# Rounding a kernel's weights two pieces at a time, turning one batch's exponentials through memory, and a new order of clamps and exponentials

## Chip, cores and metric

The kernel runs on one core of one Trainium2 chip. The metric is device microseconds of that core for one execution, the median of several runs. The engines are named PE (TensorE), DVE (VectorE), ACT (ScalarE), POOL (GpSimd) and SP (SyncE, here the queue that issues the DMAs). Each engine works through its own instructions in the order in which they are written, and waits only for data and buffers.

## What is computed

An attention block between 512 tokens and 32 state rows (8 batches, 8 heads of 64), and then a feed-forward block with a gelu over all 8 x 544 rows:

```python
scores = scale * x @ state^T;   a = softmax(scores);    xread = a @ state
scores2 = scale * state @ x^T;  a2 = softmax(scores2);  sread = a2 @ x
rows = concat([xread, sread])            # 4352 rows of 512
h = rows @ w_in                          # 512 -> 2048
g = h * (1 / (1 + exp(-1.702 * h)))
out = g @ w_out                          # 2048 -> 512
```

The arrays w_in and w_out come as 64-bit numbers (the random float32 values divided by a float64 scalar), and the kernel rounds them to float32 itself.

## The kernel before, in words

**Weights.** Both matrices are read as pairs of 32-bit words. They are cut into 32 pieces of 128 x 512 numbers (PIECES, line 180): 16 of w_in, four for each of the four 512-wide blocks w_in[0] to w_in[3], then 16 of w_out, whose pieces come as (row block f, row block f + 8) for f = 4, 5, 6, 7, 0, 1, 2, 3. A piece's raw words (512 KB) land in free rows of w_out itself (pieces 0 to 7 and 12 to 15) or in `later` (all others, room for four), by `load_weight` (184) on the SP queue. A piece is rounded by five DVE instructions of 512 elements and two of ACT: `mask` (216, L221) takes the exponent bits; `round_a` (223, L232 and L233) turns them into a power of two with two Relu on ACT, called the clamp here; `sign` (242, L245) adds the sign; `fraction` (235, L239) takes the high fraction bits; `round_b` (247, L258 and L264) adds the low word and multiplies by the power. `power` rooms are four of the six rows of `low`. Piece 18 alone has its clamp on DVE (L229, L230). `round_to` and `powers_to` say how many pieces are rounded or clamped by a place in the code; `refill` issues the next loads once the raw words in their room have been used.

**Attention.** Batches 0 and 1 are worked together at the start. `att_M(b, c)` (575) multiplies the state with w_in[c], eight PE products of 64 rows x 512 into two PSUM banks, and copies both to SBUF on ACT. `up_x(b, f)` (671, through `up`, 653) makes one 128 x 512 block of h, four PE instructions, and a gelu on ACT (L651) empties its bank; with wait=True the gelu is put on a list that `gelus(n)` (648) issues later. Softmax over the tokens: `two_s_max` (457, DVE), `two_s_exp` (467, four Exp with sums per batch, ACT, written to `room`), `two_s_norm` (485, DVE). For `att_sread` (618, 64 small PE products per batch, L629, scaled on ACT at L635) these exponentials have to be transposed. Batch 0 does it on the PE: `att_eT` (607), eight 128 x 128 transposes (L615) and two ACT copies (L616). Batch 1, and all later batches, go through memory: `eT_out` (592) writes four times 128 KB to a DRAM tile, `eT_in` (597) reads 512 KB back, and `eT_turn` (603, L605) turns 32 x 32 blocks on DVE, twice per batch.

**Banks.** PSUM has four fixed banks, bank_o[0] to bank_o[3], and two rings of two: psA (`att_ps`, tag "att") and psH (tag "h"). A tile of a ring takes a bank over from the tile two allocations before it, once all that read that one are done.

**Down product.** The loop `for i in range(HF)` at the end of the part around the change does eight steps. In step i the two pieces of rows f and f + 8 are needed (`pair_sums`, DVE sums of weights and of gelu outputs, L1479), and seven products P1 to P7 are added up in seven banks (`pair`, L1548, four PE instructions each). In step 0 stand, in this order: P1, sread of batch 0, M(1,2), three left sums, the turns of batch 1, M(1,3), rounding up to piece 19, sread of batch 1, `pair_sums`, P2, one up-product of batch 1 whose gelu is issued at once (`early`, psH), `att_srT` of both batches (a PE transpose and an ACT copy, L640 and L641), clamps up to piece 21, P6. Then P7 and P3 get their banks from psH, P4 and the later up-products from psA, and P5, P7, P3, P4 follow.

The order within each engine is that of the code; nothing else plans it.

Of the kernel before, what the change touches and what calls it, by code (L numbers as in the profile page):

```python
# [10 lines left out]
FP32 = mybir.dt.float32  # L11
# [9 lines left out]
def kernel(  # L21
# [159 lines left out]
    raw, power, begun, signed = {}, {}, {}, {}  # L181
    AHEAD = 3

    def load_weight(i):

        key = PIECES[i]
        nin, room = NFC * NPR, NF // 2
        if i < room or nin - NPR <= i < nin:
            o = 2 * (i % room if i < room else i - (nin - NPR))
            raw[i] = w_out[:, o : o + 2].rearrange("p f n -> p (f n)").bitcast(I32)  # L190
        else:
            o = 2 * (i % 4)
            raw[i] = later[:, o : o + 2].rearrange("p f n -> p (f n)").bitcast(I32)
        if key[0] == "i":
            _, c, k = key
            src = w_in_words[P * k : P * (k + 1), 2 * FC * c : 2 * FC * (c + 1)]
        else:
            src = w_out_words[P * key[1] : P * (key[1] + 1)]
        nc.sync.dma_start(raw[i], src)
# [16 lines left out]
    def mask(i):  # L216

        _, hi = words(i)
        sc = low[:, 2 + i % (AHEAD + 1)].bitcast(I32)
        power[i] = sc  # L220
        nc.vector.tensor_scalar(sc, hi, 0x7FF00000, None, ALU.bitwise_and)  # L221

    def round_a(i):

        if i not in power:
            mask(i)
        sc = power[i]
        if i == NFC * NPR + 2:
            nc.vector.tensor_scalar(sc, sc, most, least, ALU.min, ALU.max)  # L229
            nc.vector.tensor_scalar(sc, sc, -least, 8.0, ALU.add, ALU.mult)  # L230
            return
        nc.scalar.activation(out=sc.bitcast(FP32), in_=sc, func=AF.Relu, bias=edge[0], scale=-8.0)  # L232
        nc.scalar.activation(out=sc, in_=sc.bitcast(FP32), func=AF.Relu, bias=edge[1], scale=-1.0)  # L233

# [52 lines left out]

    def round_to(n, ahead=AHEAD):

        nin = NFC * NPR  # L290
        while done["b"] < min(n, len(PIECES)):
            i = done["b"]
            powers_to(i + 1)
            round_b(i, min(i + 1 + ahead, i + 3 if i > nin + 3 else i + 2 if i >= nin else nin), i >= nin or i + 1 < nin and (i + 1 < n or i >= NPR))
            done["b"] += 1
            refill()

    def piece(fill):
# [5 lines left out]
        refill()  # L304

    def pace(pieces):

        done["credit"] += pieces
        n = int(done["credit"])
        done["credit"] -= n  # L310
        round_to(done["b"] + n)


# [153 lines left out]
    def two_s_exp(b, room):  # L467
        a = A[b]
        sm = a["sm2"] = apool.tile([P, NG, 2], FP32, tag="sm4", name=f"sm4_{b}", bufs=2)
        a["e2"] = [(room[:, g], sm[:, g, :1]) for g in range(NG)]  # L470
        for g in range(NG):
            if b:

                dst = room[:, g].rearrange("p (v k i a) -> p i k v a", v=SCH, k=2, i=2)
                view = lambda t: t.rearrange("p (k v a) -> p k v a", k=2, v=SCH)
            else:
                dst = room[:, g].rearrange("p (k i q) -> p i k q", k=2, i=2)
                view = lambda t: t.rearrange("p (k q) -> p k q", k=2)
            for i in range(2):
                nc.scalar.activation(  # L480
                    out=dst[:, i], in_=view(a["s"][i][:, 2 * P * g : 2 * P * (g + 1)]), func=AF.Exp,
                    bias=a["mx2"][:, 0, g : g + 1], scale=scale, accum_out=sm[:, g, i : i + 1],
                )
# [105 lines left out]

    squares = dram.tile([SCH, Ns, NG, NPR, P], FP32, name="squares")  # L590

    def eT_out(b):
        for j in range(NPR):
            src = e2_room[b][Ns * j : Ns * (j + 1)].rearrange("n g (i q) -> n g i q", i=SCH)
            nc.sync.dma_start(squares[:, :, :, j].rearrange("i n g q -> n g i q"), src)

    def eT_in(b):

        a = A[b]
        a["eT"] = apool.tile([P, NG, SCH, P], FP32, tag="e1" if b == 1 else "eT", name=f"eT_{b}")  # L600
        nc.sync.dma_start(a["eT"].rearrange("p g j q -> p (g j q)"), squares.rearrange("i n g j q -> (i n) (g j q)"))

    def eT_turn(b, g):
        t = A[b]["eT"][:, g].rearrange("p c q -> p (c q)")
        nc.vector.transpose(t, t)  # L605

    def att_eT(b, g, spare=False):

        a = A[b]
        if g == 0:  # L610
            a["eT"] = apool.tile([P, NG, SCH, P], FP32, tag="eT", name=f"eT_{b}")
        name = f"eT_{b}_{g}"
        ps = psH.tile([P, SCH, P], FP32, tag="h", name=name) if spare else att_ps([P, SCH, P], name)
        for c in range(SCH):
            nc.tensor.transpose(ps[:, c], a["e2"][g][0][:, P * c : P * (c + 1)], ident)  # L615
        nc.scalar.copy(a["eT"][:, g], ps)  # L616

    def att_sread(b):
# [3 lines left out]
        for g in range(NG):  # L622
            for c in range(SCH):
                for j in range(NPR):
                    st = slice(Ns * j, Ns * (j + 1))
                    e, v = a["eT"][:, g, c, st], xn[b][:, NG * j + g, c]
                    if b:
                        e = a["eT"][:, g, j, Ns * c : Ns * (c + 1)]
                    nc.tensor.matmul(  # L629
# [667 lines left out]

    def rounds(n, *ahead):
        round_to(done["b"] + n, *ahead)


    load_two_states()
# [57 lines left out]
    head_exp(1)  # L1360
    fraction(NPR)
    powers_to(NPR + 2)
    up_x(0, 0, True, wait=True)
# [4 lines left out]
    for g in range(NG):  # L1368
        head_back(1, g, held[g])
    powers_to(NPR + 3)  # L1370
    piece(lambda: fraction(NPR + 1))
    up_x(0, 3, wait=True)
    gelus(2)
    powers_to(2 * NPR)
    piece(lambda: fraction(NPR + 2))
    gelus(2)

    def turn(b, c, then, n=()):

        for i in range(nper):  # L1380
            if i == nper - 1 and then:
                att_M(*then)
            up_x(b, nper * c + i)
            if i < len(n):
                rounds(n[i])

    for i in range(nper):
        up_x(1, i, i > 1, bank_o[i] if i < 2 else None)
        if 0 < i < nper - 1:
            rounds(1, 2 - i)  # L1390
            powers_to(2 * NPR + 1)
    nin = NFC * NPR
    att_M(0, 1, True)
    att_M(1, 1, banks=bank_o[:NG], copied=False)
    powers_to(2 * NPR + 2)
    def up_four(b, f):
        up_x(b, f, bank=bank_o[2 + f % 4 // 2] if f % 2 else None)

    for i in range(nper):
        up_four(0, nper + i)  # L1400
        rounds(1, 0)
        if i == 1:
            M_copies(1, 1)
        powers_to(2 * NPR + 3 + i)
    for i in range(nper):
        up_four(1, nper + i)
        if i == 1:
            att_M(0, 2)
        if i < nper - 1:
            rounds(1, 0)  # L1410
            powers_to(min(3 * NPR + 3 + i, nin))
    powers_to(nin + 1)
    up_four(0, 2 * nper)
    powers_to(nin + 2)
    room = apool.tile([P, NPR, S], FP32, tag="xT", name="e2_01")
    rounds(1, 0)
    two_s_max(1)
    late_banks = [bank_o[2], None, bank_o[3], None, bank_o[0], bank_o[1], bank_o[2]]

    def up_late(f, wait=True):  # L1420
        up_x(0, f, bank=late_banks[f - 2 * nper - 1], wait=wait)

    up_late(2 * nper + 1)
    att_M(0, 3)
    e2_room[1] = room[:, NG:]
    two_s_exp(1, e2_room[1])
    eT_out(1)
    eT_in(1)
    two_s_max(0)
    up_late(2 * nper + 2)  # L1430
    two_s_exp(0, room[:, :NG])
    up_late(2 * nper + 3)
    up_late(3 * nper)
    rounds(2, 1)
    rounds(1, 0)
    for b in (1, 0):
        two_s_norm(b)
    mask(nin + 3)
    up_late(3 * nper + 1)
    gelus(5)  # L1440
    up_late(3 * nper + 2, False)
    up_late(3 * nper + 3, False)
    for g in range(NG):
        att_eT(0, g, True)
    powers_to(nin + 4)

# [115 lines left out]
    for i in range(HF):  # L1562
        round_to(nin + 2 * i + 2)
        gelus(len(waiting))
        if i == 3:
            nc.scalar.copy(G[1, f_early // 2][:, f_early % 2], early)
        if i == 0:
            pair(i, "P1")
            att_sread(0)
            att_M(1, 2, banks=bank_o[1::2])  # L1570
            turns_of(left_sums(0))
            for g in range(NG):
                eT_turn(1, g)
            att_M(1, 3, True)
            round_to(nin + 4, 1)
            att_sread(1)
            t_room.append(pieces(apool.tile([P, NG, SCH * P], FP32, tag="eT", name="t_room_1"), 2, 2))
            s_rooms.append(four(apool.tile([P, NG, NB * Ns], FP32, tag="e1", name="s4_room")))
            pair_sums(i, left_sums(0)[3:])
            pair(i, "P2")  # L1580
            f_early = rest.pop(0)
# [3 lines left out]
            att_srT(1)  # L1585
            powers_to(nin + 6)
            pair(i, "P6")
# [158 lines left out]
```

## Time and profile before

| | us |
|---|---|
| runs | 688.04 median (687.69 to 688.35, 3 runs) |
| the profiled execution | 687.92 |
| its span, first to last instruction | 686.1 |
| PE busy | 676.9 (99%) |
| DVE busy | 558.4 (81%) |
| ACT busy | 328.0 (48%) |
| first step of the down product, P1(0), starts | 72.64 |
| second step, P1(1), starts | 85.23 |

The profile is of one execution. "Busy" is the time in which an engine worked on an instruction. A group line names the source line, the engine, the operation, output and inputs, and a time. In a timeline the first number is the start in us after the span's start, the second how long; "x4" merges that many in a row. A chain of waits goes back from the last instruction to what released each. Times of PE are overlapped by some 0.16 us from one instruction group to the next, so starts are compared and not ends.

### The profile page before, as it was taken

How to read it: one execution, taken by the hardware profiler on the slowest of the kernel's cores; microseconds unless marked ns; L12 is line 12 of the kernel's file. 1: busy time of each engine (PE TensorE's matmuls, PEld its weight loads, DVE VectorE, ACT ScalarE, POOL GpSimd, SP SyncE). 2: the span in 40 equal slices, each digit the busy share in tenths (PEclk: the TensorE clock that was granted, in tenths of full speed). 3: DMA queues.
4: the chain of work that ended last, by engine and by line, in shares of the span. 5: the costliest groups of instructions: out<-in, count | busy, mean ns of one | idle time of the engine just before them, and what ended most of it. 6: DMA issues, size and time to landing. Idle time of an engine off the chain costs nothing.

```text
span 686.1 us, 13606 instructions
## 1 busy us (share of the span) xinstructions
PE 676.9 (99%) x5347; PEld 578.0 (84%) x5347; DVE 558.4 (81%) x1066; ACT 328.0 (48%) x725; POOL 1.5 (0%) x10
## 2 busy tenths in 40 slices
PE   8999999999999999999999999999999999999996
PEld 4443687779988999889988998899988998999995
DVE  6999899999999886988878796888698885986540
ACT  7799844134355443752375335544375237421410
POOL 0000000000000000000000000000000000000000
PEclk9999999999999999999999999999999999999999
DMA  9730545338261754156443645175415640251000
GB/s 320 301 112 25 173 142 144 118 130 267 82 166 69 207 195 115 28 170 190 149 67 117 205 141 112 32 205 196 115 27 170 188 153 1 77 167 49 2 2 30
DMA packets 101391, 88.44 MB, mean 129 GB/s; under 512 B 56656, under 2 KB 80720, under 8 KB 101328
## 3 DMA queue, kind: packets, MB, share of 16 engines
q1 hardware_dynamic: 100784, 87.45, 42.6%
q8 instruction: 42, 0.69, 0.4%
q14 instruction: 21, 0.17, 0.1%
q10 hardware_dynamic: 544, 0.13, 0.1%
HBM read 69.47 MB, written 18.09 MB: 128 GB/s over the span
## 4 chain that ended last, share of the span: by engine, by line
PE 89%; DMA 4%; ACT 3%; DVE 3%; SPq 0%; issue 0%; DVEq 0%; ACTq 0%
PE low L809 28%; PE o L1219 15%; PE o L809 15%; PE upx L1219 6%; PE o L1548 4%; PE M L430 3%; PE down L1548 3%; PE o L708 3%; PE upw L1219 2%; PE o L858 2%; PE down_up L662 2%; PE h L662 1%; PE sr L629 1%; PE o L430 1%; PE upx_sr L1219 1%; ACT low L233 1%
## 5 line engine op out<-in xcount | busy, mean ns | idle before, releaser
L809 PE MATMUL low<-w_out,g_room 128*128 128x128 f32 x416 | 54.3, 276 | 0.0
L809 PEld LDWEIGHTS low<-w_out,g_room 128*128 128x128 f32 x416 | 50.5, 192 | 4.5 <-issue 4.2
L1219 PE MATMUL o<-ta,M 128*128 128x256 f32 x192 | 49.9, 382 | 0.0
L1219 PE MATMUL upx<-aT,M 128*128 128x256 f32 x192 | 49.3, 379 | 0.0
L809 PE MATMUL low<-low,g_room 128*128 128x128 f32 x336 | 43.3, 275 | 0.0
L1219 PEld LDWEIGHTS o<-ta,M 128*128 128x128 f32 x192 | 35.5, 190 | 5.9 <-ACT g_room L1265 1.6
L809 PEld LDWEIGHTS low<-low,g_room 128*128 128x128 f32 x336 | 40.3, 192 | 0.0
L1219 PEld LDWEIGHTS upx<-aT,M 128*128 128x128 f32 x192 | 36.0, 190 | 4.7
L1225 ACT ACTIVATE g_room<-o 128x512 f32<-128x512 f32 (+1 forms) x56 | 31.4, 560 | 10.4 <-PE o L1219 10.4
L809 PE MATMUL low<-sums,later 128*128 128x128 f32 x272 | 34.9, 275 | 0.0
L573 ACT COPY M<-M 128x512 f32<-128x512 f32 x53 | 27.5, 596 | 14.2 <-PE M L430 14.2
L809 PEld LDWEIGHTS low<-sums,later 128*128 128x128 f32 x272 | 32.7, 192 | 0.1
L232 ACT ACTIVATE low<-low,edge 128x512 f32<-128x512 int32 x31 | 22.5, 727 | 20.7 <-DVE low L221 20.7
L865 DVE TENSOR_TENSOR g_room<-g_room 128x512 f32<-128x512 f32 x48 | 31.7, 685 | 0.2
L1219 PE MATMUL o<-ta,ms 128*128 128x256 f32 x120 | 30.8, 379 | 0.0
L1265 ACT COPY g_room<-o 128x512 f32<-128x512 f32 (+1 forms) x28 | 15.6, 556 | 25.3 <-PE o L1219 25.3
L1225 ACT ACTIVATE g_room<-g_room 128x512 f32<-128x512 f32 (+1 forms) x28 | 16.8, 600 | 20.8 <-DVE g_room L1228 20.8
L1219 PEld LDWEIGHTS o<-ta,ms 128*128 128x128 f32 x120 | 22.8, 190 | 3.1
L1219 PE MATMUL o<-aT,m 128*128 128x256 f32 x96 | 24.6, 379 | 0.0
L809 PEld LDWEIGHTS o<-w_out,g_room 128*128 128x128 f32 x160 | 19.4, 192 | 5.0 <-issue 5.0
L430 PE MATMUL M<-w_in,stT 64*32 64x512 f32 x344 | 23.2, 592 | 0.0
L233 ACT ACTIVATE low<-low,edge 128x512 int32<-128x512 f32 x31 | 22.4, 723 | 1.1
(321 smaller groups left out, 1637.6 us busy)
## 6 DMA issues: line engine op xcount, KB each, us to landing
low<-low SPq DMA_DIRECT2D x108, 256.0 KB, 2.5
low<-low SPq DMA_DIRECT2D x11, 768.0 KB, 5.6
later<-in_moe_w_out_dram SPq DMA_DIRECT2D x16, 512.0 KB, 3.5
w_out<-in_moe_w_in_dram SPq DMA_DIRECT2D x12, 512.0 KB, 4.2
xsq<-in_x_dram SPq DMA_DIRECT2D x96, 64.0 KB, 2.2
xn<-in_x_dram SPq DMA_DIRECT2D x12, 512.0 KB, 4.2
out_dram<-osb SPq DMA_DIRECT2D x15, 256.0 KB, 2.2
squares<-e SPq DMA_DIRECT2D x28, 128.0 KB, 2.5
```

Of the source, the lines that this page charges most:

```text
L232: nc.scalar.activation(out=sc.bitcast(FP32), in_=sc, func=AF.Relu, bias=edge[0], scale=-8.0)
L233: nc.scalar.activation(out=sc, in_=sc.bitcast(FP32), func=AF.Relu, bias=edge[1], scale=-1.0)
L430: nc.tensor.matmul(ps[g][st], state_of(b, NG * j + g, g), rhs(rows, j), start=True, stop=True)
L573: nc.scalar.copy(A[b]["M", c][:, g], ps)
L662: nc.tensor.matmul(hps, lhs[i], rhs[i], start=(i == 0), stop=(i == n - 1))
L708: nc.tensor.matmul(ps[:, r], lhs[f][:, P * r : P * (r + 1)], rhs[:, f], start=(first and r == 0 and f == 0), stop=(f == HF - 1), skip_grou ...
L809: nc.tensor.matmul(ps, lhs[f], rhs[:, f], start=(first and f == 0), stop=(f == QF - 1), skip_group_check=True)
L865: nc.vector.tensor_tensor(out=out, in0=x0, in1=x1, op=op)
L1219: nc.tensor.matmul(ps[:, k], lhs[i][:, o : o + P], rhs[i], start=(first and k == 0 and i == 0), stop=(i == n - 1), skip_group_check=True,)
L1225: nc.scalar.activation(out=dst, in_=src, func=AF.Gelu_apprx_sigmoid)
L1265: nc.scalar.copy(c12, Y(u))
L1548: nc.tensor.matmul(ps7[name][:, HN * r : HN * (r + 1)], lhs[:, P * r : P * (r + 1)], rhs, start=(i == 0 and r == 0), stop=(i == HF - 1), s ...
```

## The change

- From piece 4 on, two neighbouring pieces are rounded together: each of the five DVE and two ACT instructions works on 1024 elements. The first four pieces stay single. The clamp of piece 18 on DVE is gone; all are on ACT.
- Batch 0's state exponentials go through memory like batch 1's, into a DRAM tile of their own; the PE transposes and ACT copies are gone. Both batches' maxima, exponentials, writes and reads follow one another, before M(0,3).
- The places of the rounding, of clamps, gelus and bank choices between batch 1's head and the end of the down product's first step are written anew. In step 0 the four turns now stand before the left sums, and the rounding of pair 9 after `pair_sums`, with mask and clamp of pair 10 inside and behind it.

```diff
+    def landing(i):
+        nin, room = NFC * NPR, NF // 2
         if i < room or nin - NPR <= i < nin:
+            return w_out, 2 * (i if i < room else i - (nin - NPR))
+        return later, 2 * (i % 4)
...
+    def pair_room(j):
+        return low[:, 2 + 2 * j % 4 : 4 + 2 * j % 4].bitcast(I32)
...
+    def pair_mask(j):
+        load_weights(2 * j + 2)
+        nc.vector.tensor_scalar(pair_room(j), pair_hi_lo(j)[0], 0x7FF00000, None, ALU.bitwise_and)
+
+    def pair_clamp(j):
+        clamp(pair_room(j))
+        done["a"] = 2 * j + 2
...
+    def round_pair(j, *fills):
+        hi, lo = pair_hi_lo(j)
+        dst, sc = pair_dst(j), pair_room(j)
+        nc.vector.scalar_tensor_tensor(sc, hi, -0x80000000, sc, ALU.bitwise_and, ALU.bitwise_or)
+        nc.vector.scalar_tensor_tensor(dst, lo, 2.0**-32, dst.bitcast(I32), ALU.mult, ALU.add)
+        for fn in fills:
+            fn()
+        nc.vector.scalar_tensor_tensor(dst, dst, 2.0**-20, sc.bitcast(FP32), ALU.mult, ALU.mult)
+        done["b"] = 2 * j + 2
+        raw.clear()
+        refill()
+
+    def round_next(j):
+        round_pair(j, *((lambda: pair_mask(j + 1), lambda: pair_fraction(j + 1)) if 2 * j + 2 < len(PIECES) else ()))
+        if 2 * j + 2 < len(PIECES):
+            pair_clamp(j + 1)
...
-    squares = dram.tile([SCH, Ns, NG, NPR, P], FP32, name="squares")
+    squares = [dram.tile([SCH, Ns, NG, NPR, P], FP32, name=f"squares_{i}") for i in range(2)]
...
+    pair_mask(PAIR + 1)
+    pair_clamp(PAIR + 1)
+    round_pair(PAIR, lambda: pair_fraction(PAIR + 1))
     up_x(0, 3, wait=True)
+    gelus(4)
+    pair_mask(PAIR + 2)
+    round_pair(PAIR + 1, lambda: pair_fraction(PAIR + 2))
+    up_x(1, 0, bank=bank_o[0])
+    up_x(1, 1, bank=bank_o[1])
+    pair_clamp(PAIR + 2)
+    up_x(1, 2, True, wait=True)
+    up_x(1, 3, True, wait=True)
...
     att_M(0, 1, True)
     att_M(1, 1, banks=bank_o[:NG], copied=False)
+    gelus(2)
+    pair_mask(5)
+    round_pair(4, lambda: pair_fraction(5))
+    pair_clamp(5)
+    up_four(0, nper)
+    up_four(0, nper + 1)
+    M_copies(1, 1)
+    pair_mask(6)
+    round_pair(5, lambda: pair_fraction(6))
+    pair_clamp(6)
+    up_four(0, nper + 2)
+    up_four(0, nper + 3)
+    pair_mask(7)
+    round_pair(6, lambda: pair_fraction(7))
+    pair_clamp(7)
+    up_four(1, nper)
+    up_four(1, nper + 1)
+    att_M(0, 2)
+    pair_mask(8)
+    for b in (1, 0):
+        two_s_max(b)
+    up_four(1, nper + 2)
+    pair_clamp(8)
+    up_four(1, nper + 3)
     room = apool.tile([P, NPR, S], FP32, tag="xT", name="e2_01")
+    for i, b in enumerate((1, 0)):
+        e2_room[b] = room[:, NG * i : NG * (i + 1)]
+        two_s_exp(b, e2_room[b])
+        eT_out(b)
+    for b in (1, 0):
+        eT_in(b)
+    round_pair(7, lambda: pair_fraction(8))
+    late_banks = [None, bank_o[2], None, bank_o[3], bank_o[0], bank_o[1], None, None]
...
+    for i in range(3):
+        up_late(2 * nper + i)
     att_M(0, 3)
     up_late(2 * nper + 3)
     up_late(3 * nper)
+    pair_mask(9)
+    round_pair(8, lambda: pair_fraction(9))
     for b in (1, 0):
         two_s_norm(b)
     gelus(5)
+    for i in range(1, nper):
+        up_late(3 * nper + i, False)
+    pair_clamp(9)
...
     for i in range(HF):
-        round_to(nin + 2 * i + 2)
+        if i > 1:
+            round_next(nin // 2 + i)
         gelus(len(waiting))
...
         if i == 0:
             pair(i, "P1")
-            att_sread(0)
             att_M(1, 2, banks=bank_o[1::2])
+            att_M(1, 3, True)
+            for b in (1, 0):
+                for g in range(NG):
+                    eT_turn(b, g)
             turns_of(left_sums(0))
-            for g in range(NG):
-                eT_turn(1, g)
-            att_M(1, 3, True)
-            round_to(nin + 4, 1)
-            att_sread(1)
+            for b in (1, 0):
+                att_sread(b)
...
             pair_sums(i, left_sums(0)[3:])
+            round_next(nin // 2 + 1)
             pair(i, "P2")
             f_early = rest.pop(0)
             early = xn[0].rearrange("p h c d -> p (h c d)")[:, :S]
             up_x(1, f_early, dst=early)
             att_srT(0)
             att_srT(1)
-            powers_to(nin + 6)
             pair(i, "P6")
             ps7["P7"], ps7["P3"] = (psH.tile([P, FC], FP32, tag="h", name=f"down_{k}") for k in (7, 3))
             ps7["P4"], up_bank = (att_ps([P, FC], f"down_{k}") for k in (4, "up"))
```

Pair j holds pieces 2j and 2j + 1: pairs 2 and 3 are w_in[1], 4 and 5 w_in[2], 6 and 7 w_in[3], 8 to 15 those of w_out, one for each step of the down product.

## Prediction

> **What bounds the kernel now.** I read the page's busy slices first, then the waits between 28 and 140 us (the stretch that the change touches), then the chain of waits there, then the instructions in order of time.
>
> ```profile
> PE   8999999999999999999999999999999999999996
> ...
> DVE  6999899999999886988878796888698885986540
> ```
>
> ```profile
> PEld h L662 <- ACT g_room L651: 1.6, 4, 0.8
> DVE eT L605 <- DMA eT<-squares: 1.5, 1, 1.5
> ...
> PEld sr L629 <- DVE eT L605: 1.0, 1, 1.0
> ```
>
> TensorE (PE) is the bound: from 30 us on it is busy in every slice. VectorE (DVE) is full to about 145 us too, but the PE waits for it almost nowhere. So a shorter DVE or ScalarE (ACT) instruction gives nothing by itself; only PE work or PE waits count. The place with the thinnest cover is where state exponentials come back from memory:
>
> ```profile
> 66.01 0.72 SPq L595
> ...
> 68.07 2.59 DMA squares<-e
> ...
> 70.74 5.11 DMA eT<-squares
> 75.85 0.02 issue
> 75.87 0.72 DVE eT L605
> 76.59 0.04 issue
> 76.64 1.25 PE sr L629 x64
> ```
>
> From the last exponential (66.0) to the landing of eT (75.85) are 9.85 us: write and issues 4.7, read 5.1. Next come, on ACT and on PE:
>
> ```profile
> 78.45 0.72 ACT L232 ACTIVATE low<-low,edge 128x512 f32<-128x512 int32 x1 [0.58 <-DVE low L221]
> 79.20 0.72 ACT L233 ACTIVATE low<-low,edge 128x512 int32<-128x512 f32 x1
> ...
> 80.70 0.60 ACT L651 ACTIVATE xn<-h 128x512 f32<-128x512 f32 x1 [0.37 <-PE h L662]
> 81.19 0.43 ACT L641 COPY srT<-srT 128x128 f32<-128x128 f32 x2
> 82.40 0.72 ACT L232 ACTIVATE low<-low,edge 128x512 f32<-128x512 int32 x1 [0.78 <-DVE low L221]
> ```
>
> ```profile
> 78.78 1.88 PE L662 MATMUL h<-low,M 128*128 128x512 f32 x4
> ...
> 82.64 1.03 PE L1548 MATMUL down<-w_out,g_room 128*128 128x256 f32 x4
> 83.51 1.03 PE L1548 MATMUL down<-w_out,s_room 128*128 128x256 f32 x4
> 84.37 1.03 PE L1548 MATMUL down<-t_room,sums 128*128 128x256 f32 x4
> 85.23 1.03 PE L1548 MATMUL o<-w_out,g_room 128*128 128x256 f32 x4
> ```
>
> The reader is to see: the early up-product (h at 78.78) is emptied by the gelu at 80.70, and the two products P7 and P3 (82.64, 83.51) take banks of the same two-bank ring. P3's is the third allocation after the two of M(1,3), so it is the early product's own bank. Here the gelu ends 2.2 us before P3; the clamp of 82.40 is queued behind it. P1 of the second step starts at 85.23, and from there the PE has no wait. That 85.23 is my mark.
>
> [...] one starts 0.60 after the other for L245, L258 and L264, 0.34 for L221 and L239. [...] Trace: the exponential of 1024 took 1.063. [...] Here the read of eT took 5.1 us with three loads behind it, and the first of those (71.18) landed at about 78.0: 6.8.
>
> **The change part by part.**
>
> *Pairs.* Per pair five DVE instructions go: 2 x (3 x 0.60 + 2 x 0.34) = 4.96 becomes 3 x 1.13 + 2 x 0.60 = 4.6; 14 pairs save some 5 us of DVE. A clamp (two Relu) took 1.39 from start to next on ACT; of a pair it takes 1.39 + 0.86 = 2.25 instead of 2.78. All this lies beside the PE: nothing directly. The last pair of each w_in block is ready, added up from 29.67 where head_scale ends, at 38.95 (PE needs it from 39.4), 48.5 (51.4) and 60.95 (61.2 to 61.6). So no wait takes its place.
>
> *Transposes and their copies removed.* Eight PE transposes, 71.77 to 72.64: 0.87 off the path. Two ACT copies (L616) beside the PE.
>
> *PE waits that go.* M(0,3) took 1.56 from start to next instead of 1.01, since w_in was late (0.55); the copies of M(0,1) come sooner because gelus no longer stand before them (about 0.25). So the PE reaches P1(0) at about 71.0 instead of 72.64: 1.65 earlier. The price is paid after that.
>
> *Exponentials earlier.* ACT, added up with the durations above from 30.98: clamp of pair 3, table load and four gelus end at 36.56; clamps 4 to 7 with gelus and copies between them end at 51.7; gelus and copies to 54.6; clamp 8 to 56.9; gelu 57.35; table load 1.28; four exponentials of 2.08 for batch 1 end at 60.75, those of batch 0 at 62.7. Copies of M(0,3) follow to 63.7, just in time for the up-product that needs them (63.8).
>
> *The second turn through memory.* The SP queue holds, in order: 4 writes of batch 1, 4 of batch 0, read 1, read 0, then two weight loads. Writes of batch 1 are issued 60.75 to 63.45; those of batch 0 then, landing 63.45 + 4.7 = 68.15; read 0 is issued there. Alone it would take 5.1 as in the trace. But read 1 went out 2 us before and shares the engines with the last of batch 0's writes (these ran at a DMA share of 0.99 and 194 GB/s in the trace). Bounds: 3.5 (the page's median for a 512 KB load) and 6.8 (the load that had one read in front). I take 5.6: it lands at 73.75. Four DVE turns follow (those of batch 1 done by then), 1.25 for the last two: T = 75.0. DVE had nothing from about 66 to the first landing, since its sums now stand behind the turns.
>
> *The new order after the turns.* This is where the gain is given back. DVE from T: three left sums 2.0 and the pair sums 2.08 (79.87 to 81.95 in the trace), sign 1.13, low word 1.13, mask of pair 10, 0.7: T + 7.04. Only then can ACT clamp pair 10, for 2.25, and this clamp is now queued **ahead** of the early gelu and the srT copies. Gelu ends T + 9.95, P3 starts T + 10.0. The PE itself would be there at T + 6.8 (sread 1.1, P2 0.96, up 1.72, srT 0.31, P6 0.97, P5 and P7 1.73): a wait of 3.2 that the kernel before doesn't have. P3 and P4 take 1.73: P1(1) at T + 11.7 = 86.7, against 85.23. Sum: **+1.5 us**.
>
> *After that.* DVE has the next weights at T + 8.75, T + 14.95 and T + 23.3; the PE wants them at T + 11.7, T + 17.8 and T + 25.5. So no more waits, and what is lost at 85 us is lost at the end, as the PE is full to the end. The profiled execution took 687.92 (span 686.1 and 1.8 around it): 689.4. It stands 0.12 under the median 688.04, so I forecast **689.5**.
>
> **The rivals.**
> - *Early landing:* the read takes 3.5 as a weight load does. T = 72.9, P1(1) at 84.6: -0.6, 687.4. The sign turns at T = 73.5. For it: same size and rows as a load; against: the trace's own 5.1.
> - *P3 doesn't wait (not slower):* one mechanism, the bank. If down_3 gets a bank whose reader is done, the clamp costs nothing. Then DVE decides: P1(1) at T + 8.85, P1(3) at T + 23.4 = 98.4 against 99.04: -0.65, 687.4; with an early landing -2.1, 685.9. It decides as soon as the wait at P3 is under 1.7. For it: nothing in this trace shows a wait on that bank. Against: the ring has two banks and three allocations.
> - *More waits:* P7 gets the early bank (0.86 more), the read takes 6.8 (1.2 more), or writes with a stride of eight rows into w_out make PE or DVE wait where they didn't (bounded by one step's rounding, 4.6). 690.4 to 693.
> - *The change does only what it says, work beside the PE:* then transposes and waits alone count, -1.65, 686.4; it needs both the early landing and the free bank, so it is the best end of the second rival.
>
> **How the numbers follow.** A measurement of this kernel can tell about 0.2%, 1.38 us, from no change. The worked chain (T from 74.3 to 76) has 0.50; 0.32 of that is over 1.38, 0.18 within. Early landing with the wait 0.17, nearly all within. No wait at P3 0.15: 0.08 faster, 0.07 within. More waits 0.18, slower. In all 0.09 faster, 0.41 within, 0.50 slower. The range goes from 687.2 to 691.8: it leaves out half of the free-bank case and the worst of the last one, some 0.15.
>
> **What would show it.** Right: no transposes before P1(0), which starts near 71; DVE idle before the turns until about 71; the landing of the second read near 73.8; a PE wait of about 3 us on ACT before P3; P1(1) near 86.7; DVE instructions of 1.2 for 1024 elements. Wrong: P3 without a wait, a landing under 72.3, or a PE wait for weights in later steps.

## The result, and the profile after

| kernel | median us | range | ratio to before |
|---|---|---|---|
| before | 687.99 | 687.55 to 688.35 (7 runs) | |
| after | 690.55 | 689.07 to 690.94 (7 runs) | 1.0033 [1.0022, 1.0045] |

The change makes the kernel slower by 0.33%, 2.6 us. The profiled execution took 690.55 (span 688.8, before 686.1), so it is a fair picture of the median.

The busy slices of the page, kernel after (tenths of each of 40 equal slices):

```profile
PE   8999899999999999999999999999999999999996
...
DVE  5998899989999886988969796888688885886540
```

PE still is the bound, and the slice of 69 to 86 us (the fifth) has lost a tenth. The waits of that stretch (28 to 140 us; what waited for what: us in total, times, longest):

```profile
DVE eT L626 <- DMA eT<-squares: 4.7, 2, 3.7
...
PEld down L1547 <- ACT xn L659: 2.7, 1, 2.7
...
PE down L1547 <- ACT xn L659: 2.3, 1, 2.3
...
PEld h L670 <- ACT g_room L659: 1.6, 3, 0.8
```

The weight loads (PEld) wait no more for eT, which was 1.0 before; their wait for the gelus is 1.6 as before. New is a wait of PE itself, 2.3 us: a product of the down step ("down") waits for ACT's gelu into xn, which is the early up-product's gelu. DVE's wait for eT is longer than before, 4.7 instead of 1.5, but no wait of PE for eT is left. The turns of both batches on DVE, in order of time:

```profile
70.94 1.30 DVE L626 STREAM_TRANSPOSE eT<-eT 128x512 f32<-128x512 f32 x2 [3.74 <-DMA eT<-squares]
73.24 1.31 DVE L626 STREAM_TRANSPOSE eT<-eT 128x512 f32<-128x512 f32 x2 [0.99 <-DMA eT<-squares]
74.47 0.65 DVE L1478 TENSOR_TENSOR s_room<-g_room,sums 128x512 f32<-128x512 f32 x1
```

The second read landed at 73.24, and the turns ended at 74.47. The chain of waits from there to the products (start, us, what):

```profile
78.59 1.14 DVE low L318
79.72 1.13 DVE w_out L319
80.86 0.62 DVE low L305
...
81.50 1.16 ACT low L225
...
83.73 0.59 ACT xn L659
...
84.36 3.26 PE down L1547 x8
```

Sign (L318), low word (L319) and mask (L305) on DVE, then the clamp on ACT, then the gelu, then the products: PE's start at 84.36 hangs on all of these in a row. ACT's own order shows the same from its side:

```profile
81.50 1.15 ACT L225 ACTIVATE low<-low,edge 128x1024 f32<-128x1024 int32 x1 [4.03 <-DVE low L305]
82.68 1.15 ACT L226 ACTIVATE low<-low,edge 128x1024 int32<-128x1024 f32 x1
83.73 0.58 ACT L659 ACTIVATE xn<-h 128x512 f32<-128x512 f32 x1
```

ACT did nothing for 4.03 us before the clamp, though the gelu's input was complete about 79.3 (the up-product at 77.41 took 1.88); the gelu stood behind the clamp in ACT's order. And PE:

```profile
77.41 1.88 PE L670 MATMUL h<-low,M 128*128 128x512 f32 x4
...
81.07 1.03 PE L1547 MATMUL down<-w_out,g_room 128*128 128x256 f32 x4
84.36 1.55 PE L1547 MATMUL down<-w_out,s_room 128*128 128x256 f32 x4 [2.27 <-ACT xn L659]
85.71 1.91 PE L1547 MATMUL down<-t_room,sums 128*128 128x256 f32 x4
87.42 1.49 PE L1547 MATMUL o<-w_out,g_room 128*128 128x256 f32 x4
```

P3 is the line at 84.36. From one product to the next are 1.35, 1.71 and 1.33 us here (the next one, P2, starts at 88.75), where the kernel before and every undisturbed place of this one have 0.86. The windows of the kernel after give the reason (stretch in us, its length; then busy us and instructions of PE, PEld, DVE, ACT and POOL; then the granted PE clock, the DMA share and GB/s):

```profile
82.00:84.00 2.00, 0.10 (x1) 0.00 (x0) 1.93 (x4) 1.97 (x3) 0.00 (x0) 1.00 0.90 348
84.00:85.00 1.00, 0.64 (x3) 0.59 (x4) 0.96 (x4) 0.64 (x3) 0.00 (x0) 0.97 0.73 299
85.00:86.00 1.00, 1.00 (x4) 0.81 (x3) 1.00 (x2) 0.00 (x0) 0.00 (x0) 0.50 0.03 12
86.00:87.00 1.00, 1.00 (x4) 0.72 (x4) 1.00 (x2) 0.00 (x0) 0.00 (x0) 0.50 0.00 0
87.00:88.00 1.00, 1.00 (x4) 0.81 (x3) 1.00 (x3) 0.18 (x1) 0.00 (x0) 0.50 0.00 0
88.00:89.00 1.00, 1.00 (x6) 0.83 (x5) 1.00 (x2) 0.97 (x1) 0.00 (x0) 0.83 0.83 201
```

After the wait, PE was granted half its clock for some 3.4 us. "1.00 busy" hides it; the clock column and the number of instructions (4 where 6 are usual) show it. The extra time is 1.35 + 1.71 + 1.33 - 3 x 0.86 = 1.8 us.

So the time goes as follows. P1(0) starts at 71.68, 0.96 earlier than before. P1(1) starts at 87.42, 2.19 later than before, and the last of the slow products makes it 2.66 (87.42 + 1.33 against 85.23 + 0.86). Nothing changes after that: the span has grown by 2.7.

### The profile page after: what moved, and what is told of

It is laid out like the page before. It is cut to its first block, busy times and chain, and to the rows that moved or that the text cites. A ratio compares the mean times of both kernels' runs of the same rounds, so it can differ in the third digit from the quotient of the medians.

```text
span 688.8 us, 13508 instructions
## 1 busy us (share of the span) xinstructions
PE 677.4 (98%) x5339; PEld 578.4 (84%) x5339; DVE 555.1 (81%) x996; ACT 321.2 (47%) x697; POOL 1.4 (0%) x10
## 4 chain that ended last, share of the span: by engine, by line
PE 93%; DMA 2%; DVE 2%; ACT 1%; issue 0%; DVEq 0%
PE low L817 28%; PE o L1227 15%; PE o L817 15%; PE upx L1227 6%; PE M L456 4%; PE o L1547 4%; PE h L670 4%; PE down L1547 3%; PE o L670 3%; PE o L716 3%; PE upw L1227 2%; PE o L866 2%; PE down_up L670 1%; PE o L456 1%; PE upx_sr L1227 1%; PE sr L637 1%
## 5 line engine op out<-in xcount | busy, mean ns | idle before, releaser
L225 ACT ACTIVATE low<-low,edge 128x1024 f32<-128x1024 int32 (+1 forms) x18 | 19.1, 1062 | 23.5 <-DVE low L305 20.4
L873 DVE TENSOR_TENSOR g_room<-g_room,later 128x512 f32<-128x512 f32 x35 | 22.8, 683 | 0.0
```

Of the source, the lines that this page charges most:

```text
L873: nc.vector.tensor_tensor(out=out, in0=x0, in1=x1, op=op)
```

## The experiments

My theory: the early gelu's place behind the clamp makes P3 wait, and the wait itself costs a second time through the clock. Against it stood that the loss isn't tied to that place in ACT's order, but to something else in this stretch, and that the low clock has another cause than the idle time. Each kernel is set against runs of the kernel before on the same chip; what is compared is the ratio.

| kernel | median us | before, same chip | ratio |
|---|---|---|---|
| clamp of pair 10 behind the gelu | 687.29 | 687.95 | 0.9992 [0.9984, 1.0001] |
| left sums ahead of the turns | 688.08 | 687.95 | 1.0003 [0.9994, 1.0011] |
| both | 686.45 | 687.95 | 0.9978 [0.9969, 0.9986] |
| two added products | 689.04 | 687.95 | 1.0018 [1.0010, 1.0026] |
| pairs in halves | 693.66 | 687.82 | 1.0077 [1.0059, 1.0095] |
| batch 0 turned on PE | 688.86 | 687.82 | 1.0015 [1.0008, 1.0022] |
| batch 0 on PE, and both moves | 687.44 | 687.82 | 0.9995 [0.9987, 1.0003] |
| the kernel before, its clamp moved ahead | 688.07 | 687.82 | 1.0005 [0.9997, 1.0013] |
| both moves, pairs in halves | 689.02 | 688.10 | 1.0015 [1.0009, 1.0022] |

### The clamp behind the gelu

```diff
-            round_next(nin // 2 + 1)
+            j = nin // 2 + 1
+            round_pair(j, lambda: pair_mask(j + 1), lambda: pair_fraction(j + 1))
             pair(i, "P2")
...
             att_srT(0)
             att_srT(1)
+            pair_clamp(j + 1)
             pair(i, "P6")
```

> The changed kernel with one step moved: the clamp of pair 10 stands on ACT behind the early gelu and the two srT copies instead of ahead of them. Theory A (P3 waits for the early product's bank, whose gelu is queued behind that clamp, and the PE runs slowly after the wait): the wait of 2.27 us before P3 is gone, the granted clock stays at 1.00 there, P3 starts near 82.0, P1(1) near 83.7, and P1(3), which then waits a little for DVE, near 97.9 instead of 101.69: 686.8, about 3.8 below the changed kernel and 1.2 below the kernel before. Rival B (weights rounded in pairs come too late): the PE only waits elsewhere, at P1(1), and the time stays within 1 us of the changed kernel.

Measured: 687.29. PE of this kernel around the same place, and where the fourth step begins:

```profile
81.06 1.03 PE L1547 MATMUL down<-w_out,g_room 128*128 128x256 f32 x4
81.92 1.03 PE L1547 MATMUL down<-w_out,s_room 128*128 128x256 f32 x4
...
83.65 1.03 PE L1547 MATMUL o<-w_out,g_room 128*128 128x256 f32 x4
...
98.10 1.13 PE L1547 MATMUL o<-w_out,g_room 128*128 128x256 f32 x4 [0.34 <-DVE w_out L322]
```

P3 follows P7 after 0.86 with no wait, and no product of this stretch is stretched. The place of one clamp in ACT's order thus carries the whole loss of the kernel after, some 3 us, and the theory that it lies elsewhere falls. The interval holds 1: this kernel is level with the one before. The clamp itself was done 81.66 to 83.99 and nobody missed it: DVE wanted it at 84.98. What limits this kernel a little is the fourth step's weights (0.34 at 98.10).

### The left sums ahead of the turns

```diff
             att_M(1, 3, True)
+            turns_of(left_sums(0))
             for b in (1, 0):
                 for g in range(NG):
                     eT_turn(b, g)
-            turns_of(left_sums(0))
```

> The changed kernel with the three left sums of step 0 ahead of the four turns on DVE, into the time in which DVE waits for the first landing; the clamp stays where it is. Theory A: turns end at the same 74.5, mask of pair 10 comes 2.0 us earlier, P3 waits only about 0.3 us, the clock isn't lowered: P1(1) near 84.1, 686.8, about 3.8 below the changed kernel. Rival B: DVE ends 2 us earlier, so weights come 2 us earlier and the gain is at most 2.0: 688.5.

Measured: 688.08, between the 686.8 that I expected and the rival's 688.5. DVE had some 3.7 us without work before the first landing, so I expected to fill them with sums for nothing. DVE's second sum in this kernel, and then PE:

```profile
71.73 0.69 DVE L1478 TENSOR_TENSOR s_room<-s_room,g_room 128x512 f32<-128x512 f32 x1 [2.05 <-PE h L670]
```

```profile
83.75 1.13 PE L1547 MATMUL down<-w_out,s_room 128*128 128x256 f32 x4 [1.52 <-ACT xn L659]
84.72 1.03 PE L1547 MATMUL down<-t_room,sums 128*128 128x256 f32 x4
85.58 1.03 PE L1547 MATMUL o<-w_out,g_room 128*128 128x256 f32 x4
```

The second sum's output takes memory that the last up-product still reads, so it had to wait for PE until 71.7, and the turns behind it ended at 75.85 instead of 74.47. The clamp began at 80.88, only 0.62 earlier than in the kernel after. But the wait at P3 fell from 2.27 to 1.52, and with that the slow products vanished: P4 and P1(1) come after 0.97 and 0.86. None of its 13 runs has a mean clock under 0.998, where five of the seven of the kernel after have. Of the gain of 1.84 us at P1(1) (87.42 to 85.58), 0.61 is the earlier P3, and the rest is the clock.

### Both moves

The two diffs above together.

> Both moves: clamp of pair 10 behind the copies, left sums ahead of the turns. Theory A: no wait at P3, and DVE 2 us ahead, so also none at P1(3): P1(3) near 97.5, 686.3, some 1.7 below the kernel before. Rival B: as the second of these runs, 688.5.

Measured: 686.45, as expected, and less than both kernels: 0.22% under before, with an interval that leaves out 1. ACT's order at the place:

```profile
79.27 0.60 ACT L659 ACTIVATE xn<-h 128x512 f32<-128x512 f32 x1 [1.86 <-PE h L670]
...
80.47 1.15 ACT L225 ACTIVATE low<-low,edge 128x1024 f32<-128x1024 int32 x1 [0.28 <-DVE low L305]
```

The gelu runs when its input is there (released by PE, not by ACT's own queue), 4.5 us earlier than in the kernel after. PE has no wait from P1(0) to the end of the down product; P1(1) starts at 83.60, 1.63 earlier than before, and the fourth step at 97.41 without the wait of the first experiment.

### Two added products

```diff
             ps7["P7"], ps7["P3"] = (psH.tile([P, FC], FP32, tag="h", name=f"down_{k}") for k in (7, 3))
+            for _ in range(2):
+                nc.tensor.matmul(ps7["P7"], ident, w_in[0][:, 0], start=True, stop=True)
             ps7["P4"], up_bank = (att_ps([P, FC], f"down_{k}") for k in (4, "up"))
```

Two 128 x 512 products are added whose result P7 overwrites; everything else is the kernel after. They take PE's time where it would wait anyway, and shorten only the idle stretch.

> The changed kernel with two more 128x512 products of no use before P5 of step 0, written to P7's bank, which P7 then starts afresh: 1.72 us of PE work inside the wait before P3. Theory A: P3 starts at the same 84.4 (it waits for ACT), but the PE was idle for only some 0.5 us, so the granted clock stays at 1.00 and P3, P4 and P1(1) take 0.86 each: P1(1) at 86.1, 688.8, about 1.8 below the changed kernel. Rival C (the lower clock has another cause than the idle time): P3, P4 and P1(1) stay slow, 690.5 or, if the added work isn't hidden, more.

Measured: 689.04. Its PE:

```profile
84.14 1.13 PE L1547 MATMUL down<-w_out,s_room 128*128 128x256 f32 x4 [0.72 <-ACT xn L659]
85.10 1.03 PE L1547 MATMUL down<-t_room,sums 128*128 128x256 f32 x4
85.97 1.03 PE L1547 MATMUL o<-w_out,g_room 128*128 128x256 f32 x4
```

P3 starts about when it did (84.14 against 84.36), yet P4 and P1(1) follow at full pace and P1(1) comes 1.45 earlier. Useless work on PE brings the kernel from 1.0033 to 1.0018 of the time before; the two intervals overlap by a little, but in the trace the pace of P3, P4 and P1(1) is not in doubt, and none of the 13 runs has a mean clock under 0.997. So the low clock here is a consequence of the idle time, not of the traffic or the products themselves.

### Pairs in halves

Every DVE and ACT instruction of a pair is issued as two of 512 elements, in the same places:

```diff
     def pair_mask(j):
         load_weights(2 * j + 2)
-        nc.vector.tensor_scalar(pair_room(j), pair_hi_lo(j)[0], 0x7FF00000, None, ALU.bitwise_and)
+        for k in range(2):
+            nc.vector.tensor_scalar(half(pair_room(j), k), half(pair_hi_lo(j)[0], k), 0x7FF00000, None, ALU.bitwise_and)
...
```

> The changed kernel with every instruction on a pair (five on DVE, two on ACT) done as two on 512 elements, all else in its place. Theory A (the time is set by the chain clamps, exponentials, second landing, turns, sums, mask of pair 10, clamp, early gelu, P3): a pair's clamp takes 2.78 instead of 2.25 on ACT, so the exponentials come some 1.6 us later after what ACT's own waits absorb, and the last mask and clamp another 0.7: the wait before P3 grows from 2.3 to about 4.5, with the lower clock after it: 692.8, about 2.3 above the changed kernel. Rival (wide instructions lie beside the PE and are worth nothing, or cost time by coming in larger steps): 690.5 or less.

Measured: 693.66. PE:

```profile
86.96 2.08 PE L1557 MATMUL down<-w_out,s_room 128*128 128x256 f32 x4 [3.71 <-ACT xn L669]
88.83 1.91 PE L1557 MATMUL down<-t_room,sums 128*128 128x256 f32 x4
90.53 1.90 PE L1557 MATMUL o<-w_out,g_room 128*128 128x256 f32 x4
```

The wait is 3.71, less than the 4.5 that I expected, but the slow stretch is twice as long: it lasts to about 92 (clock 0.50 in every window from 86 to 92). It isn't met each time: of the six runs, two have a mean clock of 1.000 and took 690.94 and 691.78, the other four 0.993 to 0.995 and 693.27 to 695.28. P1(0) already starts 1.15 later than in the kernel after, at 72.83. In the new order the width of the instructions does lie on the path: DVE and ACT stand between the turns and P3 with all their length.

### Both moves, pairs in halves

The same halves on top of both moves. Is the width worth anything once P3 doesn't wait?

> Both moves (clamp behind the copies, left sums ahead of the turns), and every instruction on a pair done as two on 512 elements. Theory A: with the wait at P3 gone, halves cost only what the PE waits for ahead of the down product (P1(0) starts 1.15 later, as it did with halves before) and perhaps 0.3 for weights in step 3: 687.9, some 1.5 above the same kernel with whole pairs and the same as the kernel before. Rival (pairs lie beside the PE and are worth nothing once P3 doesn't wait): 686.5.

Measured: 689.02, 0.37% over the kernel with both moves when each is set against its own runs of before. More than I expected. PE of this kernel, in an execution of 689.72, somewhat above the median:

```profile
72.97 1.03 PE L1557 MATMUL o<-w_out,g_room 128*128 128x256 f32 x4
...
85.31 1.03 PE L1557 MATMUL o<-w_out,g_room 128*128 128x256 f32 x4
...
159.35 1.16 PE L827 MATMUL o<-low,spare_M 128*128 128x128 f32 x8 [0.80 <-ACT o L836]
163.43 1.16 PE L827 MATMUL o<-low,later 128*128 128x128 f32 x8 [0.23 <-DVE spare_M L832]
```

P3 has no wait here either, but P1(0) starts 1.35 later than with whole pairs (71.62), P1(1) 1.71 later, and after the down product two waits on ACT and DVE take another 1.03. Together 2.7 of the 3.2 us by which its span (687.9) exceeds that of the kernel with both moves (684.7); the rest is spread. So the time that wide instructions save on DVE and ACT is a reserve, which this order uses up in three places.

### Batch 0 turned on PE

The kernel after, but batch 0's exponentials are turned by eight PE transposes and two ACT copies behind the last up-product, and only batch 1 goes through memory:

```diff
...
+        if b:
+            eT_out(b)
+            eT_in(b)
...
+    for g in range(NG):
+        att_eT(0, g)
     pair_clamp(9)
...
-            for b in (1, 0):
-                for g in range(NG):
-                    eT_turn(b, g)
+            for g in range(NG):
+                eT_turn(1, g)
```

> The changed kernel with batch 0's exponentials turned by eight PE transposes and two ACT copies again, behind the last up-product; batch 1 still goes through memory. Theory A: turns end near 72.4 instead of 74.5, mask of pair 10 comes 2.1 us earlier, and the PE is 0.87 later: no wait before P3, which starts near 82.8; P1(1) near 84.6 instead of 87.4: 687.2, about 3.3 below the changed kernel although the PE does more. Rival (the transposes taken from the PE are a plain gain of 0.87): 691.4.

Measured: 688.86. I expected no wait at P3, since the turns would end early. They did, at 71.03, 3.4 us before those of the kernel after. One line of DVE says where that went, one of PE what was left:

```profile
76.60 0.43 DVE L1496 TENSOR_TENSOR sums<-w_out 128x256 f32<-128x256 f32 x1 [3.39 <-PE sr L653]
```

```profile
84.53 1.13 PE L1565 MATMUL down<-w_out,s_room 128*128 128x256 f32 x4 [1.05 <-ACT xn L675]
```

The first of the pair sums is written to memory (sums) from which sread of batch 1 still reads its input on PE. It began at 76.60, against 76.44 in the kernel after, early as the turns were. But the transposes themselves delay that sread: it starts at 75.89 here and at 74.52 in the kernel after. The memory came free 0.71 after it started (76.60 - 75.89); an estimate from this for the kernel after is 75.2, so that there an early landing could bring the pair sums forward by at most 1.2. P3's wait is shorter only because PE itself came 1.4 later (P7 at 82.45 against 81.07: the transposes and what stands around them). At 1.05 us of wait the clock held (1.00 in every window from 80 to 94).

### Batch 0 turned on PE, with both moves

> Both moves of the third of the earlier runs (clamp behind the copies, left sums ahead of the turns), and batch 0 turned by the PE. Theory A: the PE waits nowhere in either, so here the eight transposes count in full: 0.9 above that run's 686.45, 687.3. Rival (landing and turns still cost time when nothing waits at P3): equal to it or below, 686.4.

Measured: 687.44, 0.99 over the kernel with both moves alone; by the ratios, since the chips differ, 1.2. P3 has no wait in its profile (83.06, P7 at 82.20), and P1(1) starts at 84.79, 1.19 later than with the turn through memory (83.60). Eight transposes cost 0.87 and a wait for their bank 0.25. So when PE never waits, the transposes count in full, and taking them off PE is worth about 1 us. That part of the change does what it should.

### The kernel before, its clamp moved ahead

In the kernel before, `powers_to(nin + 6)` goes from behind `att_srT(1)` to ahead of `pair(i, "P2")`, so that there too a clamp (one of 512) stands before the early gelu.

> The kernel before with a single move: the clamp of piece 21 stands on ACT ahead of the early gelu and the srT copies instead of behind them. Theory A: its mask is there at 82.4, the clamp ends near 83.9, the early gelu at 84.4, and P3 starts at 84.5 instead of 83.5: about 1.0 above the kernel before, 688.9; the PE idle for less than 1 us, so the clock stays. Rival (the bank of P3 isn't the early product's): 688.0.

Measured: 688.07 against 687.82; the interval holds 1. ACT:

```profile
81.90 0.72 ACT L232 ACTIVATE low<-low,edge 128x512 f32<-128x512 int32 x1 [1.67 <-DVE low L221]
...
83.28 0.58 ACT L651 ACTIVATE xn<-h 128x512 f32<-128x512 f32 x1
```

The gelu came 2.6 us later, at 83.28 instead of 80.70, but PE came later as well in this execution, and P3, at 83.91, stood only 0.05 behind its turn. The 688.9 that I expected did not come, and the rival's 688.0 did, but without a wait at P3 the test decides nothing; the bank is shown by the first experiment.

## Why the prediction was right, and where its working was not

It forecast 689.5, in a range from 687.2 to 691.8, with slower as the likeliest sign, at 0.50; measured were 690.55 and slower. The range is wide, and two of the rivals (687.4 each) lie in it too, so the times inside the trace say more than the number. The mechanism was the one that it put down as the worked chain, and the first experiment shows it by taking it away. Some terms of the sum were off, and one was missing.

**The head.** *P1(0) at about 71.0*: 71.68. Of the 0.7, 0.3 had been there since 29.6, before anything I worked out. The rest is M(0,3), which took 1.40 to the next instruction instead of 1.01: its last weights came at about 62.0, while my sum had them at 60.95. "So no wait takes its place" was wrong by 0.4.

**The exponentials and the second turn.** Batch 1's ended at 61.5 (forecast 60.75), batch 0's at 63.4 (62.7). The second read landed at 73.24 (73.75), and T was 74.47 (75.0). That these agree so well is in part luck. The read's line on the SP queue is

```profile
69.23 0.33 SPq L622 DMA_DIRECT2D eT<-squares  x1
```

It was issued 1.1 later than my 68.15, and took 4.0 instead of the 5.6 that I chose between my bounds. My rival of an *early landing* took all of DVE's work as following from T, and did not see that the pair sums need memory which sread of batch 1 reads: with batch 0 on PE, batch 1's read was issued at 66.45 and had landed by 69.80, and yet the pair sums began no earlier. With the turn through memory that bound is weaker, near 75.2 by the estimate above, where the rival had 72.9 + 2.0 = 74.9; no run shows it.

**The new order.** *Clamp at T + 7.04*: T + 7.03. *P3 at T + 10.0*: T + 9.89. The 1.13 and 0.60 for 1024 elements on DVE were my estimates; they are what the trace has from start to start (1.13 to 1.14 and 0.6 in the chain above). The 0.86 for the wider clamp on ACT was one too: the clamp took 2.23 to the next instruction (81.50 to 83.73), where I had 2.25. The wait was 2.27 and not 3.2: P3 came 0.64 earlier than the forecast 85.0, and PE would have started P3 at 81.93 (P7 at 81.07, plus 0.86), 0.13 later than the forecast T + 6.8 = 81.8. Counted from start to start that is a wait of 2.43; the trace's 2.27 counts from P7's end. In the sum one sread lay behind T; in the trace PE was at M(1,3) until T, and both sreads came after.

**The step that failed.** "P3 and P4 take 1.73" was read from the kernel before. They took 3.06, and P1(1) another 0.47 too much. The term was 1.8 us too small because I priced the wait with its length alone. I had taken my 3.2 us for a wait and nothing more; in the trace a wait of 2.27 is followed by a clock of 0.50. The waits of 0.72, 1.05 and 1.52 in the experiments cost nothing of that kind: the clock is 1.00 in every window around them.

When the clock falls can be read from windows of a tenth of a us. First the kernel after, then the one with pairs in halves (columns as in the windows above, the clock third from the end):

```profile
84.90:85.00 0.10, 0.10 (x2) 0.10 (x1) 0.10 (x2) 0.00 (x0) 0.00 (x0) 0.67 0.21 82
...
685.60:685.70 0.10, 0.00 (x0) 0.00 (x0) 0.00 (x0) 0.00 (x0) 0.00 (x0) 0.90 0.00 0
```

```profile
85.40:85.50 0.10, 0.00 (x0) 0.00 (x0) 0.10 (x1) 0.10 (x1) 0.00 (x0) 0.77 0.89 369
...
689.60:689.70 0.10, 0.00 (x0) 0.00 (x0) 0.00 (x0) 0.00 (x0) 0.00 (x0) 0.56 0.15 20
```

In the kernel after the clock falls at 84.93 (two thirds of that tenth are at 0.50) and rises at 88.35, 3.4 us later. With halves it falls at 85.45, while the PE still waits, and rises at 92.28, 6.8 us later. At the end of both executions, where the PE has run out of work, it falls once more, at 685.68 and 689.61. So the fall does not keep to one place in the wait: in the kernel after it comes 0.57 us after P3 has started (84.36), with halves 1.51 before (86.96). By then the PE had idled for 2.27 us in the kernel after and for 2.20 with halves (83.25 to 85.45); in the profiles where the clock stayed, the longest wait was 1.52. What sets the moment isn't shown.

The slow stretch fits the differences between runs of one kernel: the four slowest of the kernel after (690.55 to 690.94) have a mean clock of 0.995, the two fastest (689.07 and 689.36) one of 0.998. With halves it is plainer: 6.8 us at half clock make a mean of 0.995 or less, so the two runs with 1.000 can't have had them. What spared these runs isn't shown.

**The sum.** Against my 86.7 at P1(1), T gave back 0.5 and the step to P3 0.1, and the slow P3 and P4 took 1.33: 87.42. The slow P1(1) took 0.47 more. 689.4 + 0.7 + 0.5 = 690.6, which is what the profiled execution took. Two errors of opposite sign did not cancel; the one that I hadn't seen was the larger. Without the slow stretch the same execution would have taken some 688.7 (690.55 - 1.8, an estimate), so my 689.5 lies between the two cases and describes neither.

**The rival "P3 doesn't wait".** It was priced at P1(1) at T + 8.85 and the fourth step at T + 23.4. In the first experiment T was 74.63, so 83.48 and 98.03; measured were 83.65 and 98.10, and 687.29 where the rival said 687.4. The bank decides as it was put down. At the fourth step the PE did wait for DVE, as the rival had it; at P1(1) it did not, and the agreement there is luck. The prediction gives two figures for the rival's best end, 685.9 and, as *only work beside the PE*, 686.4; they don't agree with each other. The kernel with both moves has 686.45 and a gain of 1.63 at P1(1), which is close to the second (1.65) by luck: the 1.65 was to lie ahead of P1(0), where the gain is 1.02 (71.62 against 72.64); the other 0.61 comes between P1(0) and P1(1), 11.98 instead of 12.59. It needs no early landing (turns until 75.44): the sums ahead of the turns do the same service.

**Pairs.** "All this lies beside the PE: nothing directly" is not what the halves show: to split each instruction again costs 2.5 us with both moves, and 3 us in the kernel after. Part of the 3 is the longer slow stretch; the two runs of each that I take to be without one (690.94 and 691.78 against 689.07 and 689.36) are some 2 apart. With halves even the kernel with both moves is no faster than the kernel before (1.0015), so the new order needs the wide instructions.

What stays open: how much idle time it takes (1.52 us did not do it, 2.20 did), what sets the moment of the fall, and how often an execution meets it. The stride with which pairs are written into w_out was a rival's detail that no run set apart; DVE's 1.22 us for such a write and for one into `low` are alike.

## What to carry to other kernels

When work is moved on an engine that isn't the bound, look at each buffer that the bound engine takes next, and ask what now stands ahead of that buffer's last reader in its engine's order; a release that was two us early can become two us late though the releasing instruction is the same. Price a wait on PE as long as the 2.27 us here twice, once for its length and once for the slow products that may follow it (1.8 us here), and rather place the instruction that releases it first. And before counting on an earlier input, list every memory that the waiting instruction writes: the next reader in line may hold it anyway.

## What the runs showed of the hardware

The granted PE clock fell to 0.50 after 2.27 us without work and stayed there for 3.4 us, which cost 1.8 us; with a wait of 3.71 it stayed for 6.8, and waits up to 1.52 us did not do it. The fall came 0.57 us after work had started again in the kernel after, and 1.51 before that with halves, when the PE had idled for 2.20. Two products of no use, placed before P5 so that the gap shrank to 0.72, brought the pace back: 0.96, 0.87 and 0.86 us from one product to the next from P3 on. The same read of 512 KB, with weight loads behind it in each, took 3.35 us in the kernel with batch 0 on PE, 4.0 in the kernel after and 5.1 in the kernel before; what makes the difference stays open.
